# Two head pairs loaded four tokens to a partition, one set of squares split between two engines, and the operands of the last matmul stage made later

## The chip, the core and the metric

The kernel runs on one core of a Trainium2 chip. The metric is the time of one execution on the device in microseconds (us). The engines are named as in the profile: PE is TensorE (PEld its weight loads), DVE is VectorE, ACT is ScalarE, POOL is GpSimd, SP is SyncE, which here only issues DMAs.

## What is computed

The reference is an attention block with normalised queries and keys, followed by a feed-forward block with the activation SoLU.

```
q_n, k_n = rmsnorm(q, g_q), rmsnorm(k, g_k)         # q, k, v: (8, 12, 448, 64)
attn = softmax(q_n @ k_n.T / 8);  x = (attn @ v)    # -> x: (3584, 768)
h = x @ w_in                                        # w_in: (768, 1024)
solu = h * softmax(h)
ln = (solu - mean) / sqrt(var + 1e-6) * g_ln
out = ln @ w_out                                    # w_out: (1024, 768)
```

All data are float32 (the weights arrive as float64).

## The kernel before

**Attention, 0 to about 315 us.** The 96 heads are worked as 48 pairs; two pairs make a quad, so there are 24 quads. For each pair the scores are made in three blocks of 128 keys (`scores`, L802) and one block of the last 64 keys of both pairs of a quad (`scores_last`, L815). ACT takes the exponentials out of PSUM (L792), PE multiplies them with the values (L848, L859) and sums them with matmuls with ones (L881). PSUM has three buffers for score blocks, so a fourth block waits until the exponentials of the first have been taken.

Queries and keys must be normalised and transposed before the scores. From pair 2 on this runs on several engines: `squares` (ACT, L662), `row_sums` (DVE, L670), `fold_sums` (POOL, L680 and L681), `rsqrt_seed` (ACT, L687 and L688), `rsqrt_step` (DVE, L694 to L697), `normalise` (POOL, L703), `qk_transpose` (DVE, L713), `gain` (ACT, L717). The first two pairs take a shorter way: `load_rows` (L728) loads each head with tokens j*112+p in partition p, so in runs of one token (64 floats, 256 bytes), `square_rows` and `sum_rows` (L738, L740, L746) make the sums, `normalise_rows` (L762) scales the rows in place, `transpose_rows` (L768) transposes four 112x128 blocks with PE, and `take_rows` (L774 to L778) copies the result out of PSUM into `qkT`.

The order on each engine is the order in which the program issues the instructions: the attention's first quad is written out by hand (the branch `m == 0` of the loop), with `unit(...)` marking a piece of PE work.

**First feed-forward matmul, to about 569 us.** 28 tiles of 128 rows are worked as 14 groups of two tiles. Each group is a 2x2 block product that is made with seven half-size products instead of eight (p1 to p7 in `products`, L980), in banks A, B, C and D of PSUM, each with 6 matmul records and about 2.58 us. DVE adds the partial results and takes row maxima (`plus`, L996). When half a group is finished, `done` puts five steps of the activation on a list of due times (`later`): `ff_exp` (ACT, L1051), `ff_mult` (DVE, L1055), `ff_moments` (DVE L1063 to L1068, then POOL L1069 and L1071), `ff_norm` (ACT, L1075) and `ff_spread` (DVE transpose L1084, then four DMAs to DRAM, L1087). The due times are counted in PE pieces; the last two groups have due times of their own. The tiles concerned are tile 25 and 24 (group 12, its second and first half) and tile 27 and 26 (group 13).

**Second feed-forward matmul, the last stage, from 569 us.** It works on seven blocks n = 0 to 6 of four tiles, again with seven products instead of eight on two levels: the outer products P1, P5, P6, P2, P7, P3, P4 (in that order, q = 0 to 6 of each block), and in each of them seven inner products at `PLACES = (0, 4, 8, 10, 12, 16, 20)` slots after the start of the outer one, with `STEP = 7` slots from one outer product to the next. From slot 21 on there is one inner product in every slot. An inner product is four matmul records (L1194) and takes 0.65 us when PE runs freely. Numbered by their order on PE from the start of the stage, products 0, 1, 3, 4, 6, 9 and 13 belong to P1 (p1, p2, p6, p5, p7, p4, p3), products 2, 5, 8, 10, 12, 16 and 20 to P5, products 7, 11, 15, 17 and 19 to P6 (p1, p2, p6, p5, p7). From slot 21 on the number is the slot less 7.

Inner products accumulate into a bank that an engine reads in between: in P1 and P5 ACT copies bank A (L1206), in the others DVE adds to it (L1208); DVE makes the results out of C, B and B (L1233 for p2, L1246 for p7, L1256 for p3). So p6, p7 and p4 of an outer product wait for the reading of bank A, and p3 waits for the reading of bank B by p7.

The operands of a block come from DRAM (`load_u`, L1131, on SP's queue behind the spreads that were issued before) and are made by `make`: a11, a12 and a22 are copies on ACT (L1149, L1151, L1153), s1, s2, s3 and s4 are sums or differences on DVE (L1155, L1157, L1159, L1161), each in two halves t = 0 and 1. `inner_sums` (POOL, L1172 to L1175) forms the four sums of an operand that p6, p5, p7 and p3 use. `made(n, name, slots)` says in which slots the two halves are issued.

Of the kernel before, what the change touches and what calls it, by code (L numbers as in the profile page):

```python
# [14 lines left out]
OP = AluOpType  # L15
# [351 lines left out]
def fast_path(  # L367
# [274 lines left out]
    def load_v(m, queue=nc.sync):  # L642
# [14 lines left out]
        d["vl"] = lasts.pop(m)  # L657

    def squares(n):
        d = st[n]  # L660
        d["sq"] = work.tile([P, 2 * NB, 32], FP32, tag="sq", name="sq", bufs=2)
        nc.scalar.activation(d["sq"].rearrange("p (s b) d -> p s (b d)", s=2), d["qk"], AF.Square)  # L662
# [59 lines left out]
    def load_rows(n, queues):  # L722
        b, hp = divmod(n, NP)
        d = st[n] = {}
        d["qk"] = xs.tile([P, 2, 4, P], FP32, tag="x", name="x")[0:R]
        for s, src in enumerate((q, k)):
            for h in range(2):
                queues[2 * s + h].dma_start(  # L728
                    d["qk"][:, s, :, h * D : (h + 1) * D], src[b, 4 * (hp // 2) + hp % 2 + 2 * h].rearrange("(j p) d -> p j d", p=R)
                )  # L730

    def square_rows(n, s, engine):
        d = st[n]
        if s == 0:
            d["sq"] = xs.tile([P, 2, 4, P], FP32, tag="x", name="xsq")[0:R]
        x, y = d["qk"][:, s], d["sq"][:, s]
        if engine is nc.scalar:
            nc.scalar.activation(y, x, AF.Square)  # L738
        else:
            engine.tensor_tensor(y, x, x, OP.mult)  # L740

    def sum_rows(n, s):
        d = st[n]
        if s == 0:
            d["ss"] = small.tile([P, 4 * NB], FP32, tag="ss", name="ss", bufs=2)[0:R, 0:16]
        nc.vector.tensor_reduce(  # L746
            d["ss"][:, s * 8 : s * 8 + 8], d["sq"][:, s].rearrange("p j (h d) -> p (j h) d", h=2), AX, OP.add
        )

    def warm_up():  # L750
# [4 lines left out]
        for _ in range(5):  # L755
            nc.tensor.matmul(o, w[:, 0:P], w, start=True, stop=True)

    def normalise_rows(n, s):
        d = st[n]
        x = d["qk"][:, s].rearrange("p j (h d) -> p (j h) d", h=2)  # L760
        y = d["y"][:, s * 8 : s * 8 + 8].rearrange("p i -> p i ()").to_broadcast([R, 8, D])
        nc.vector.tensor_tensor(x, x, y, OP.mult)  # L762

    def transpose_rows(n, s):
        d = st[n]
        d["pt", s] = ps_t.tile([P, S], FP32, tag="o", name="pt", bufs=2)
        for j in range(4):
            nc.tensor.transpose(d["pt", s][:, j * R : (j + 1) * R], d["qk"][:, s, j], ident[0:R, 0:R])  # L768

    def take_rows(n, s):  # L770
        d = st[n]
        if s == 0:
            d["qkT"] = work.tile([P, 2, S], FP32, tag="qkT", name="qkT", bufs=3)
            nc.scalar.activation(d["qkT"][:, 0], d["pt", 0], AF.Copy, scale=gcol[:, KF : KF + 1])  # L774
        elif n == 0:
            nc.scalar.copy(d["qkT"][:, 1], d["pt", 1])
        else:
            nc.vector.tensor_copy(d["qkT"][:, 1], d["pt", 1])  # L778

# [312 lines left out]
    def in_parts():  # L1092
        def done(g, i):
            t = 2 * g + i
            ff_max(t)
            waits = {
                (NG - 2, 1): (1, 2, 3, 5, 5), (NG - 1, 1): (1, 2, 3.25, 6.75, 7), (NG - 1, 0): (2.25, 3.75, 4.75, 7.5, 8)
            }.get((g, i), (1, 2, 3, 5, 7))
# [45 lines left out]
    def make(n, name, t):  # L1144
# [11 lines left out]
        elif name == "s2":  # L1156
            nc.vector.tensor_tensor(o, us[n, "s1"][:, t], us[n, "a11"][:, t], OP.subtract)  # L1157
        elif name == "s3":
# [195 lines left out]
    with tc.manual_schedule():  # L1354
# [19 lines left out]
        for m in range(NQ):  # L1374
# [18 lines left out]
            if m == 0:  # L1393
# [3 lines left out]
                unit(lambda: scores(a, 1))  # L1397
                unit(lambda: scores(a, 2))
                for s in range(2):
                    transpose_rows(1, s)  # L1400
                    take_rows(1, s)
                squares(2)
                add(a)
                add_more(a)
                row_sums(2)
                unit(lambda: scores_last(m))
                squares(3)
                unit(lambda: scores(b, 0))
                row_sums(3)
                fold_sums(1)  # L1410
                unit(lambda: scores(b, 1))
                unit(lambda: scores(b, 2))
                add(b)
                norms_next()
                squares(4)
                row_sums(4)
# [138 lines left out]
        for n in range(NS):  # L1555
            base = period * n
            for i, name in enumerate(ORDER):
# [5 lines left out]
                if q > 1:  # L1563
                    when(STEP * q - 6, lambda n=n, x=x: inner_sums(n, x))
            for x, t, slot in (("V", 1, 31), ("V", 0, 34), ("C22", 1, 45), ("C22", 0, 52)):
# [115 lines left out]
```

## Time and profile before

| | us |
|---|---|
| median of 3 runs (lowest, highest) | 807.04 (806.71, 807.82) |
| the profiled execution, its own time | 807.2 |
| its span, first to last instruction | 805.4 |
| PE busy | 789.7 |
| DVE busy | 612.8 |
| POOL busy | 519.9 |
| ACT busy | 473.0 |

The profile is of one execution. Times in it count from the start of the span. In a timeline line the first number is the start, the second the duration from the first to the last of the instructions that the line merges, then come engine, line, operation and what is written from what; the bracket at the end tells how long the engine sat idle before and which event ended that. In the view of stretches each engine's busy time is given with its number of instructions, then the granted PE clock (1.00 is full speed), the busy share of the DMA engines (over 1 where packets overlap) and the rate.

### The profile page before, as it was taken

Reading aid. Unit: us, or ns where it says so; the run is one execution under the profiler, and the core shown is the slowest. Engines: PE = TensorE matmul, PEld = TensorE weight load, DVE = VectorE, ACT = ScalarE, POOL = GpSimd, SP = SyncE. Lnnn points to the kernel's source line nnn. Section 1 sums busy time; section 2 is a strip of 40 time slices with the busy share of each in tenths; the row PEclk is TensorE's granted clock in tenths of the full one; section 3 lists DMA queues with packets and bytes.
Section 4 is the critical chain, followed back from the end, with each engine's and each line's share of the span. In section 5 each row is a group of like instructions: output and inputs, shape, how many; then the busy total and the mean of one; then the engine's idle time right before and its main releaser. Section 6 shows DMA issues by size and latency. Waiting matters only on the chain.

```text
span 805.4 us, 14271 instructions
## 1 busy us (share of the span) xinstructions
PE 789.7 (98%) x4854; PEld 464.5 (58%) x4854; DVE 612.8 (76%) x1203; ACT 473.0 (59%) x783; POOL 519.9 (65%) x662
## 2 busy tenths in 40 slices
PE   8999999999999999999999999999899999999997
PEld 4344444443444433444444444444699999999996
DVE  6787989989888896488778667776886776866945
ACT  6677878878778764467767544453505455464420
POOL 2666777778777775244466466678487777777861
PEclk9999999999999999999999999999999999999999
DMA  9878899897787832555545445542647457366312
GB/s 170 159 168 156 182 194 184 196 187 161 165 160 169 161 103 66 140 131 151 150 131 147 102 119 140 141 110 52 210 125 252 133 188 267 117 229 213 120 60 83
DMA packets 269598, 122.68 MB, mean 152 GB/s; under 512 B 187596, under 2 KB 254668, under 8 KB 269516
## 3 DMA queue, kind: packets, MB, share of 16 engines
q1 hardware_dynamic: 254332, 111.78, 55.7%
q10 hardware_dynamic: 15184, 9.90, 4.5%
q8 instruction: 40, 0.66, 0.3%
q14 instruction: 42, 0.34, 0.1%
HBM read 84.94 MB, written 36.70 MB: 151 GB/s over the span
## 4 chain that ended last, share of the span: by engine, by line
PE 88%; DVE 3%; DMA 2%; SPq 2%; POOL 2%; ACT 1%; issue 1%; DVEq 0%; ACTq 0%; POOLq 0%
PE A L1194 15%; PE A L980 13%; PE o L859 12%; PE s L802 12%; PE B L980 8%; PE B L1194 8%; PE C L980 4%; PE sm L881 4%; PE D L980 4%; PE C L1194 4%; PE s L815 2%; PE o L848 2%; SPq L636 1%; DMA ur<-ud 1%; DMA xg<-xd 1%
## 5 line engine op out<-in xcount | busy, mean ns | idle before, releaser
L792 ACT ACTIVATE E<-s 128x896 f32<-128x896 f32 x168 | 138.8, 939 | 8.9 <-PE s L802 8.1
L802 PE MATMUL s<-qkT 64*64 64x448 f32 x1152 | 120.1, 545 | 1.7 <-ACT qkT L717 1.0
L859 PE MATMUL o<-E,v 128*64 128x448 f32 x576 | 113.8, 543 | 0.0
L1069 POOL TENSOR_TENSOR he<-he,mhalf 128x1 f32<-128x1 f32 x28 | 27.6, 986 | 105.6 <-DVE he L1068 95.7
L1194 PE MATMUL B<-w_out,sums 128*128 128x192 f32 x392 | 80.6, 329 | 3.3 <-DVE P L1256 2.1
L802 PEld LDWEIGHTS s<-qkT 64*64 64x64 f32 x1152 | 48.1, 163 | 60.0 <-ACT E L792 29.2
L1194 PE MATMUL A<-w_out,sums 128*128 128x192 f32 x392 | 80.6, 329 | 1.0 <-POOL sums L1175 0.7
L859 PEld LDWEIGHTS o<-E,v 128*64 128x64 f32 x576 | 39.1, 137 | 72.2 <-issue 68.0
L703 POOL TENSOR_TENSOR qkn<-qk,ny 128x896 f32<-128x896 f32 x46 | 77.1, 1697 | 3.5 <-DMA qk<-in_q_dram 1.5
L838 POOL TENSOR_TENSOR es<-es,E 128x896 f32<-128x896 f32 x22 | 46.4, 2109 | 48.9 <-ACT sq L662 35.4
L980 PE MATMUL B<-w_in,xsum 128*128 128x512 f32 x168 | 76.7, 593 | 0.5 <-POOL he L1069 0.5
L980 PE MATMUL A<-w_in,xg 128*128 128x512 f32 x168 | 74.6, 593 | 0.0
L1194 PEld LDWEIGHTS B<-w_out,sums 128*128 128x128 f32 x392 | 66.9, 191 | 3.9 <-DVE P L1256 2.4
L1051 ACT ACTIVATE u<-h,hmax 128x1024 f32<-128x1024 f32 x28 | 32.1, 1148 | 62.7 <-DVE hmax L1045 62.7
L1194 PEld LDWEIGHTS A<-w_out,sums 128*128 128x128 f32 x392 | 66.8, 191 | 1.7 <-POOL sums L1175 1.6
L980 PEld LDWEIGHTS B<-w_in,xsum 128*128 128x128 f32 x168 | 31.8, 190 | 41.0 <-issue 39.0
L980 PEld LDWEIGHTS A<-w_in,xg 128*128 128x128 f32 x168 | 31.8, 190 | 40.1 <-issue 39.3
L829 DVE TENSOR_TENSOR es<-E 128x896 f32<-128x896 f32 x48 | 53.0, 1107 | 2.1 <-ACT E L792 2.1
L670 DVE TENSOR_REDUCE part<-sq 128x28 f32<-128x896 f32 x46 | 47.9, 1080 | 4.4 <-ACT sq L662 2.0
L680 POOL COPY ss<-part 32x56 f32<-32x56 f32 x92 | 46.8, 508 | 6.7 <-DVE part L670 2.2
L713 DVE STREAM_TRANSPOSE qkT<-qkn 128x896 f32<-128x896 f32 x46 | 48.4, 1087 | 0.4 <-POOL qkn L703 0.4
L1194 PE MATMUL A<-w_out,s 128*128 128x192 f32 x224 | 45.6, 326 | 0.0
(150 smaller groups left out, 1647.8 us busy)
## 6 DMA issues: line engine op xcount, KB each, us to landing
ur<-ud SPq DMA_DIRECT2D x60, 256.0 KB, 4.7
ud<-ub SPq DMA_DIRECT2D x112, 128.0 KB, 2.3
xd<-xo SPq DMA_DIRECT2D x48, 224.0 KB, 3.0
qk<-in_q_dram SPq DMA_DIRECT2D x92, 112.0 KB, 3.2
qk<-in_k_dram SPq DMA_DIRECT2D x92, 112.0 KB, 3.0
v<-in_v_dram SPq DMA_DIRECT2D x24, 384.0 KB, 4.4
out_dram<-P SPq DMA_DIRECT2D x19, 384.0 KB, 4.3
raw<-in_moe_w_in_dram SPq DMA_DIRECT2D x12, 512.0 KB, 5.5
```

The costliest lines, as they stand in the source:

```text
L670: nc.vector.tensor_reduce(norms[m]["part"][:, i], st[n]["sq"], AX, OP.add)
L680: e.tensor_copy(ss[g * 32 : g * 32 + 32], part[o * 32 : o * 32 + 32])
L703: e.tensor_tensor(d["qkn"].rearrange("p (s b) d -> p s b d", s=2), d["qk"].rearrange("p s (b d) -> p s b d", d=32), y.rearrange("p (s b) - ...
L713: nc.vector.transpose(d["qkT"].rearrange("p s t -> p (s t)"), d["qkn"].rearrange("p b d -> p (b d)"))
L792: nc.scalar.activation(d["E", kc], s[:, :, 0:S], AF.Exp)
L802: nc.tensor.matmul(s[c : c + D, h, 0:S], d["qkT"][hh, 1, keys], d["qkT"][hh, 0, :], start=True, stop=True,)
L829: nc.vector.tensor_tensor(d["es"], d["E", 0], d["E", 1], OP.add)
L838: e.tensor_tensor(d["es"], d["es"], d["E", 2], OP.add)
L859: nc.tensor.matmul(d["o"][h * D : (h + 1) * D, :], quads[n // 2]["v"][:, n % 2 + 2 * h, kc], d["E", kc][:, h], start=False, stop=(kc == NJ ...
L881: nc.tensor.matmul(sm[g : g + 32, :], ones[:, w], e[:, h, t * S // 2 : (t + 1) * S // 2], start=(x == 0), stop=(x == len(terms) - 1),)
L980: nc.tensor.matmul(k[bank], a[:, c], w_in[i][:, c], start=begin and c == 0, stop=c == HD - 1, skip_group_check=not begin,)
L1194: nc.tensor.matmul(k[bank], a[:, c].rearrange("p a i -> p (a i)"), w_out[:, area, i, c], start=begin and c == 0, stop=c == KC - 1, skip_gr ...
```

## The change

1. `load_rows` puts tokens 4p to 4p+3 of a head into partition p, so a run is four tokens (1 KB). The tile's layout is (head, token, d) instead of (token, head, d). `normalise_rows` no longer works in place: it writes into the tile of the squares, in the layout that the transposes need. `take_rows` restores the order of the tokens as it copies out of PSUM, by writing each element four elements (16 bytes) after the one before.
2. In the first quad, `squares(3)` (one ACT instruction over q and k) becomes two instructions: the half for q on DVE, ahead of `take_rows` of pair 1, and the half for k on ACT, right behind `squares(2)`. `row_sums(3)` and `fold_sums(1)` are issued before `scores(b, 0)`, and `scores(b, 2)` after the seeds of the norms of the next quad, so that its exponentials follow the seeds on ACT. PE's order is the same.
3. For the last tiles of the first feed-forward matmul the due times move: moments, norm and spread of tile 24 from 3, 5, 7 to 4, 6, 7; the spread of tile 27 from 7 to 7.25; mult, moments, norm and spread of tile 26 from 3.75, 4.75, 7.5, 8 to 4.25, 6.75, 8, 8.75.
4. s2 of block 0 is made on POOL instead of DVE. Its second half is issued in slot 1 instead of 3, and the inner sums of P6 of block 0 in slot 5 instead of 8.
5. The operands of block 1 are issued later: s1 in slots 39 and 41 instead of 27 and 30, s2 in 43 and 45 (34 and 38), s3 in 47 and 49 (40 and 42), s4 in 51 and 53 (47 and 49), a22 in 55 and 57 (53 and 55). a11 and a12 stay.

```diff
+    def squares_half(n, s, vector):
+        d = st[n]
+        if s == 0:
+            d["sq"] = work.tile([P, 2 * NB, 32], FP32, tag="sq", name="sq", bufs=2)
+        y, x = d["sq"].rearrange("p (s b) d -> p s (b d)", s=2)[:, s], d["qk"][:, s]
+        if vector:
+            nc.vector.tensor_tensor(y, x, x, OP.mult)
+        else:
+            nc.scalar.activation(y, x, AF.Square)
...
-        d["qk"] = xs.tile([P, 2, 4, P], FP32, tag="x", name="x")[0:R]
+        d["qk"] = xs.tile([P, 2, 2, 4, D], FP32, tag="x", name="x")[0:R]
...
-                    d["qk"][:, s, :, h * D : (h + 1) * D], src[...].rearrange("(j p) d -> p j d", p=R)
+                    d["qk"][:, s, h], src[...].rearrange("(p j) d -> p j d", p=R)
...
+    def flat(x):
+        return x.rearrange("p h j d -> p (h j d)")
+
     def normalise_rows(n, s):
         d = st[n]
-        x = d["qk"][:, s].rearrange("p j (h d) -> p (j h) d", h=2)
-        y = d["y"][:, s * 8 : s * 8 + 8].rearrange("p i -> p i ()").to_broadcast([R, 8, D])
-        nc.vector.tensor_tensor(x, x, y, OP.mult)
+        y = d["y"][:, s * 8 : s * 8 + 8].rearrange("p (h j) -> p h j ()", h=2).to_broadcast([R, 2, 4, D])
+        o = flat(d["sq"][:, s]).rearrange("p (j h d) -> p h j d", h=2, d=D)
+        nc.vector.tensor_tensor(o, d["qk"][:, s], y, OP.mult)
...
-            nc.scalar.activation(d["qkT"][:, 0], d["pt", 0], AF.Copy, scale=gcol[:, KF : KF + 1])
+        to = d["qkT"][:, s].rearrange("p (r j) -> p j r", j=4)
+        pt = d["pt", s].rearrange("p (j r) -> p j r", j=4)
+        if s == 0:
+            nc.scalar.activation(to, pt, AF.Copy, scale=gcol[:, KF : KF + 1])
         elif n == 0:
-            nc.scalar.copy(d["qkT"][:, 1], d["pt", 1])
+            nc.scalar.copy(to, pt)
         else:
-            nc.vector.tensor_copy(d["qkT"][:, 1], d["pt", 1])
+            nc.vector.tensor_copy(to, pt)
...
-                (NG - 2, 1): (1, 2, 3, 5, 5), (NG - 1, 1): (1, 2, 3.25, 6.75, 7), (NG - 1, 0): (2.25, 3.75, 4.75, 7.5, 8)
+                (NG - 2, 1): (1, 2, 3, 5, 5), (NG - 2, 0): (1, 2, 4, 6, 7),
+                (NG - 1, 1): (1, 2, 3.25, 6.75, 7.25), (NG - 1, 0): (2.25, 4.25, 6.75, 8, 8.75),
...
-            nc.vector.tensor_tensor(o, us[n, "s1"][:, t], us[n, "a11"][:, t], OP.subtract)
+            (nc.vector if n else nc.gpsimd).tensor_tensor(o, us[n, "s1"][:, t], us[n, "a11"][:, t], OP.subtract)
...
                 unit(lambda: scores(a, 2))
+                squares_half(3, 0, True)
                 for s in range(2):
                     transpose_rows(1, s)
                     take_rows(1, s)
                 squares(2)
+                squares_half(3, 1, False)
                 add(a)
                 add_more(a)
                 row_sums(2)
                 unit(lambda: scores_last(m))
-                squares(3)
-                unit(lambda: scores(b, 0))
                 row_sums(3)
                 fold_sums(1)
+                unit(lambda: scores(b, 0))
                 unit(lambda: scores(b, 1))
-                unit(lambda: scores(b, 2))
                 add(b)
                 norms_next()
+                unit(lambda: scores(b, 2))
                 squares(4)
...
-                    when(STEP * q - 6, lambda n=n, x=x: inner_sums(n, x))
+                    when(STEP * q - 6 if q > 2 else 5, lambda n=n, x=x: inner_sums(n, x))
...
-            late = 6 if n == 1 else 0
-            made(n, "a11", base + 12 + late, base + 15 + late)
-            made(n, "s1", base + 21 + late, base + 24 + late)
-            made(n, "s2", base + 28 + late, base + 38)
+            late = n == 1
+            made(n, "a11", base + 12 + 6 * late, base + 15 + 6 * late)
+            made(n, "s1", base + 21 + 18 * late, base + 24 + 17 * late)
+            made(n, "s2", base + 28 + 15 * late, base + 38 + 7 * late)
             made(n, "a12", base + 33, base + 36)
-            made(n, "s3", base + 40, base + 42)
-            made(n, "s4", base + 47, base + 49)
-            made(n, "a22", base + 53, base + 55)
+            made(n, "s3", base + 40 + 7 * late, base + 42 + 7 * late)
+            made(n, "s4", base + 47 + 4 * late, base + 49 + 4 * late)
+            made(n, "a22", base + 53 + 2 * late, base + 55 + 2 * late)
...
-        made(0, "s2", 0, 3)
+        made(0, "s2", 0, 1)
```

More of the change, by code (lines that the diff above doesn't have):

```diff
@@ L728, in load_rows @@
                 queues[2 * s + h].dma_start(
-                    d["qk"][:, s, :, h * D : (h + 1) * D], src[b, 4 * (hp // 2) + hp % 2 + 2 * h].rearrange("(j p) d -> p j d", p=R)
+                    d["qk"][:, s, h], src[b, 4 * (hp // 2) + hp % 2 + 2 * h].rearrange("(p j) d -> p j d", p=R)
                 )
@@ L734, in square_rows @@
         if s == 0:
-            d["sq"] = xs.tile([P, 2, 4, P], FP32, tag="x", name="xsq")[0:R]
+            d["sq"] = xs.tile([P, 2, 2, 4, D], FP32, tag="x", name="xsq")[0:R]
         x, y = d["qk"][:, s], d["sq"][:, s]
@@ L746, in sum_rows @@
         nc.vector.tensor_reduce(
-            d["ss"][:, s * 8 : s * 8 + 8], d["sq"][:, s].rearrange("p j (h d) -> p (j h) d", h=2), AX, OP.add
+            d["ss"][:, s * 8 : s * 8 + 8], d["sq"][:, s].rearrange("p h j d -> p (h j) d"), AX, OP.add
         )
@@ L767, in transpose_rows @@
         for j in range(4):
-            nc.tensor.transpose(d["pt", s][:, j * R : (j + 1) * R], d["qk"][:, s, j], ident[0:R, 0:R])
+            nc.tensor.transpose(d["pt", s][:, j * R : (j + 1) * R], flat(d["sq"][:, s])[:, j * P : (j + 1) * P], ident[0:R, 0:R])
     def take_rows(n, s):
```

## The prediction

> **What bounds the kernel now.** I read the page's first part, then who PE waited for, then the stretches and timelines around those waits.
>
> ```profile
> span 805.4 us, 14271 instructions
> PE 789.7 (98%) x4854; PEld 464.5 (58%) x4854; DVE 612.8 (76%) x1203; ACT 473.0 (59%) x783; POOL 519.9 (65%) x662
> ```
>
> PE is busy for all but 805.4 - 789.7 = 15.7 us, so the change can win only there, or where PE is busy at a low clock. PE's waits:
>
> ```profile
> PE B L1194 <- DVE P L1256: 2.1, 1, 2.1
> PE s L815 <- ACT E L792: 1.3, 2, 0.7
> PE pt L768 <- DVE x L762: 1.2, 1, 1.2
> PE B L1194 <- DVE P L1246: 1.2, 1, 1.2
> PE s L802 <- ACT qkT L717: 1.0, 1, 1.0
> PE A L1194 <- POOL sums L1175: 0.7, 1, 0.7
> PE s L802 <- ACT qkT L776: 0.6, 1, 0.6
> PE B L980 <- POOL he L1069: 0.5, 1, 0.5
> ```
>
> The L1194 and L980 rows lie between 566 and 598 us, where the last stage begins; the rest, but for one of the two at L815, lies before 30 us. From 30 to 300 us PE waits for nothing. The stretches at the first two show one thing more:
>
> ```profile
> 582.00:584.00 2.00, 0.20 (x2) 0.00 (x0) 2.00 (x5) 1.15 (x2) 1.82 (x4) 1.00 0.28 108
> 584.00:586.00 2.00, 1.65 (x8) 1.65 (x9) 1.71 (x5) 0.42 (x1) 2.00 (x3) 0.83 0.48 110
> 586.00:588.00 2.00, 2.00 (x8) 2.00 (x7) 0.67 (x2) 0.00 (x0) 1.92 (x4) 0.50 0.86 207
> 588.00:590.00 2.00, 2.00 (x11) 2.00 (x11) 1.47 (x4) 0.74 (x2) 1.99 (x3) 0.82 0.55 207
> ```
>
> The reader is to see PE idle while DVE is full, and then a granted clock of 0.50: products 18 to 21 start at 585.10, 586.16, 587.44 and 588.72, so three steps take 3.62 instead of 3 x 0.65 = 1.95 us. The wait of 2.15 costs a further 1.67. What kept DVE:
>
> ```profile
> 581.69 0.68 DVE L1161 TENSOR_TENSOR s<-a,s 128x512 f32<-128x512 f32 x1
> 582.29 0.34 DVE L1233 TENSOR_TENSOR P<-C,q 128x192 f32<-128x192 f32 x1
> 582.56 0.34 DVE L1246 TENSOR_TENSOR P<-B,u 128x192 f32<-128x192 f32 x1
> 582.82 1.23 DVE L1084 STREAM_TRANSPOSE ub<-u 128x1024 f32<-128x1024 f32 x1
> 583.98 0.31 DVE L1256 TENSOR_TENSOR P<-B,u 128x192 f32<-128x192 f32 x1
> ```
>
> Bank B is read (L1256) only behind a spread; before that came moments, mult(26) and two s2.
>
> **What the Trainium skill says.** "TensorE: Matmul & The Clock Gate", section on the HAM clock gate: PE falls to half clock after an idle window of about 3.4 us and returns after a busy one. The trace agrees on half (0.50) and about 3.5 us; here 2.15 us of waiting, 1.16 shortly before it, were enough. "SBUF — State Buffer", Who interferes with whom: a DVE instruction with two SBUF inputs and a POOL instruction that reads SBUF block each other. Agrees: the power at L1069 takes 0.55 us alone and 1.46 under a DVE product (559.84). The same page, Door 1, on 16-byte lines: an access that crosses to a new line pays. No row of before writes so; reading every second word costs ACT 820 against 630 ns (L535, L536, 128x512). "DMA: Bandwidth & Descriptors", Why small descriptors are slow: fixed work per packet. Agrees in direction: 251 to 281 GB/s at full DMA share from 2.5 to 4 us with runs of 256 bytes, 354 and 379 at 568 to 570 with long rows.
>
> **Part 1, the loads.** The first pair's four DMAs carry 448 KB: about 1.75 us at 260 GB/s, 1.25 at 360, so DVE's first square (4.45) starts 0.5 earlier. The chain from there to the first score (10.46) has that much room beside it: the gain column's transpose is held by PE's warm-up to 7.2, and ACT's squares of pair 1, which follow it, end at 8.64, where the first copy would start at 9.32 - 0.5 = 8.82. Given back: two copies on the path (0.63 and 0.53) write with a step of 16 bytes. At the 30% of L535 over L536 that is +0.17 each; bounds nothing and doubling. The new output layout of L762 is in whole runs of 64: nothing. Sum +0.2 (from -0.7 to +0.7).
>
> **Part 2, the squares.** DVE is free from 12.89 to 13.93, which hides 0.6 for half the squares; without that cover it would delay L778. The other half (some 0.5) ends on ACT at 15.95 and puts the exponentials of the last keys from 15.71 to 15.95; PE's third block of pair 1, released at 16.68, loses about 0.2. That lies before the 1.0 wait at 26.02 and is absorbed by it. Row sums of pair 3 move from 17.50 to 16.55; the fold (18.73) is then held by POOL's add until 17.81; the seeds go from 20.97 to about 20.1. Late next: the exponentials of L792 for `scores(b, 2)`, 0.92, now stand behind the seeds, so the squares of pair 4 stay at 21.67, their row sums end at 23.74, and the transpose behind them goes from 24.16 only to 23.75. Sum +0.45 (0 to 0.8). The following wait of 0.66 at 29.28 hangs on the same chain and moves along.
>
> **Part 3, due times of tile 24.** B's first reading (L996) comes before the moments: at 564.53, when ACT has copied u3, instead of 566.08. PE goes on at 566.40 instead of 566.92 and the last stage starts at 568.98 instead of 569.57: +0.59. On ACT exp(27) now precedes norm(24), which ends at 570.46 instead of 568.43; the copy of q behind it stays at 570.4, and product 3 (570.93) just gets it.
>
> **Parts 3 and 4, products 9 to 21.** With before's steps DVE runs: mult(27) 570.11, p2 571.25, spread(24) 571.52, moments(27) 572.68, two s3 574.61, p2 575.81, p7 of P1 576.07 to 576.42. Product 13 needs that at 577.4: the wait of 1.16 goes. s2 costs POOL two of about 1.34 us (L563, 128x512), where POOL was idle from 567.2 to 576.6; even blocked by mult(27) and starting only after the last in-stage matmul it is ready by 573, and product 7 wants its first half at 573.5. Then mult(26), s4, p2 end at 578.6. P5's p7 needs ACT's copy of u3, queued behind a11 of block 1, whose load follows spread(24), 1.7 earlier than before: about 579.3. P1's p3 is done by 579.6, product 17 starts at 580.4: the wait of 2.15 goes, and 1.67 of low clock with it.
>
> Late next, two new waits. ACT's a12 copies wait for a load that lands at 573.65 (issued behind spread(25), not moved); the copy of u3 behind them ends at 575.16, and product 9 now wants it at 574.83: -0.35. And product 19 (581.7) waits for DVE's reading of P6's A (L1208), behind spread(27) 1.16, s4 0.6, one add 0.27: about 581.9, a microsecond more if a11 lands late: -0.6 (0.2 to 1.0).
>
> **Part 5, block 1's operands.** The 0.66 at product 33 goes (its release at 597.32 is DVE's L1208 behind a V and an s2; the profile names POOL). The work comes back in slots 39 to 55: 17 adds at 0.28 start to start = 4.8, s1, s2, s3, s4 twice at 1.02, 0.96, 0.68, 0.82 = 7.0, two C22 at 0.8 = 1.6; 13.4 us, where PE needs 16 x 0.65 = 10.4. Of the 3.0 about 2 is room, as a bank is read some three slots before it is wanted. -0.9 (0 to 1.6). The operands have more than 6 us to their use, so POOL's sums and the loads they release are covered.
>
> **Sum.** Stage: 0.59 + 1.16 + 2.15 + 1.67 + 0.66 - 0.35 - 0.6 - 0.9 = 4.4 (3.3 to 5.7). Start: 0.65. Together 5.05, from the profiled execution's own 807.2 (span 805.4 and 1.8 around it) to 802.15; its time is 0.16 above the median 807.04, so 802.0.
>
> **Rivals.** *All clean* (0.13): POOL's blocking and the strided writes cost nothing, products 19 and 45 never wait: stage 5.9, start 1.3, so 799.8. For it: before, DVE passed a similar crowd at 589 to 606 with one wait of 0.66. *The backlog reaches the clock* (0.19): in slots 45 to 58 DVE and POOL stretch each other (s2 1.21 where 0.68 is possible), PE waits 2 us within one window and pays another 1.67: 804.3. For it: 13.4 against 10.4 us. *Hidden anyway, the change doesn't do what it says* (0.06): the loads of block 1 land so late that P5's u3 copy and with it L1256 are as late as before; only 0.6 and the start remain: 806. Against it: spread(24) moves with its norm, which was never the late one. *Slower* (0.04): DVE stays the bound of products 13 to 21, so that all of the stage's 4.4 is lost, and the operands packed into slots 39 to 55 add 1.5 of waits and a second half-clock window of 1.67: 807.0 + 3.2 - 0.65 = 809.6. It decides from 2 us of PE idle within one such window (2.15 did it, 1.16 alone not).
>
> **Chances.** Forecast 0.58, its own range 800.8 to 803.2. Range 799.8 to 804.8: the forecast, most of the backlog case and half of the clean one, 0.8. Faster by over 0.2% (about what a measurement of this kernel can tell from no change), below 805.4: 0.58 + 0.19 + 0.13 = 0.90; same 0.06; slower 0.04.
>
> **What would show it.** Right: the L1256 and L1246 rows gone from PE's waits, clock 1.00 throughout 578 to 592, the last stage beginning about 1.2 earlier, waits of under 0.5 at products 9 and 19. Wrong: a wait over 1 us between products 38 and 51, a clock below 1 there, copies at `take_rows` over 0.9 us, POOL's s2 over 2 us each.

## The result and the profile after

The changed kernel takes 803.26 us, the median of 13 runs (801.98 to 806.14), against 807.18 for the kernel before beside it (13 runs, 805.98 to 808.20). The ratio is 0.9956, 95% interval 0.9946 to 0.9965: faster by 3.9 us, where 5.05 was forecast. The profiled execution took 802.73 with a span of 800.9, so that one is 4.47 below the profiled execution of before.

The page's first part. PE is busy as long as before to within 0.6 us, in a shorter span; POOL's busy time has grown by 3.8:

```profile
span 800.9 us, 14266 instructions
PE 789.1 (99%) x4854; PEld 462.8 (58%) x4854; DVE 613.8 (77%) x1202; ACT 473.1 (59%) x783; POOL 523.7 (65%) x664
```

PE's waits, all that the view lists: time in all, times, longest (line numbers are those of the changed kernel; L818 and L831 are the scores, L1211 the last stage's products, L1273 and L1263 the readings of bank B that were L1256 and L1246, L1225 the reading of A that was L1208):

```profile
PE s L818 <- ACT qkT L792: 1.6, 1, 1.6
PE pt L766 <- DVE warm L763: 1.4, 1, 1.4
PE s L831 <- ACT E L808: 0.9, 2, 0.7
PE A L1211 <- POOL sums L1190: 0.8, 1, 0.8
PE A L1211 <- DVE u L1225: 0.6, 2, 0.4
PE B L1211 <- DVE P L1273: 0.5, 1, 0.5
PE s L831 <- ACT qkT L790: 0.3, 1, 0.3
PE pt L781 <- DVE xsq L775: 0.2, 1, 0.2
PE s L818 <- ACT qkT L727: 0.2, 1, 0.2
```

The rows of 2.1 and 1.2 at bank B are gone. At the start waiting has moved more than it has gone: PE's wait for the copy of the first pair grew from 0.6 to 1.6, while the rows of 1.2 before the transposes and of 1.0 at pair 2 shrank to 0.2 each. The stretches at the old waits:

```profile
582.00:584.00 2.00, 1.43 (x9) 1.46 (x10) 1.93 (x7) 0.00 (x0) 1.86 (x3) 1.00 0.85 204
584.00:586.00 2.00, 2.00 (x14) 2.00 (x13) 1.93 (x8) 0.65 (x1) 1.50 (x3) 1.00 0.79 254
586.00:588.00 2.00, 2.00 (x14) 2.00 (x13) 1.77 (x4) 1.61 (x3) 1.92 (x4) 1.00 0.18 70
588.00:590.00 2.00, 2.00 (x15) 2.00 (x14) 1.93 (x6) 0.00 (x0) 1.92 (x4) 1.00 0.56 124
```

The clock stays at 1.00 where it was 0.50, and in the stretch from 582 PE stands still for 0.57 us instead of 1.80, although DVE is as full as before. The timeline shows why: P1's reading of B now comes ahead of the spread.

```profile
578.67 0.62 ACT L1166 COPY a<-ur 128x512 f32<-128x512 f32 x1 [1.14 <-DMA ur<-ud]
579.20 0.31 ACT L1223 COPY u<-A 128x192 f32<-128x192 f32 x1
579.54 0.36 DVE L1263 TENSOR_TENSOR P<-B,u 128x192 f32<-128x192 f32 x1
579.82 0.35 DVE L1273 TENSOR_TENSOR P<-B,u 128x192 f32<-128x192 f32 x1
580.08 1.24 DVE L1100 STREAM_TRANSPOSE ub<-u 128x1024 f32<-128x1024 f32 x1
```

Product 17 then starts at 580.32 instead of 584.35. The last stage's first product starts at 568.58 (569.57 before) and its last at 794.72 (799.29), 4.57 earlier. Of that 0.22 was there before the stage's eve: PE's block that began at 558.50 begins at 558.28. It isn't the start's doing, as PE's wait for exponentials at 29 us ends later than before (29.43, not 29.28); a wait near 306 us, of which more below, was 0.39 shorter in this execution. The remaining 4.35 come from the stage and its eve.

### The profile page after: what moved, and what is told of

Same layout as the page of the kernel before. It is cut to its first block, busy times and chain, and to the rows that moved or that the text cites. A ratio compares the mean times of both kernels' runs of the same rounds, so it can differ in the third digit from the quotient of the medians.

```text
span 800.9 us, 14266 instructions
## 1 busy us (share of the span) xinstructions
PE 789.1 (99%) x4854; PEld 462.8 (58%) x4854; DVE 613.8 (77%) x1202; ACT 473.1 (59%) x783; POOL 523.7 (65%) x664
## 4 chain that ended last, share of the span: by engine, by line
PE 88%; DVE 4%; POOL 2%; ACT 2%; DMA 1%; issue 1%; SPq 0%; DVEq 0%; ACTq 0%; POOLq 0%
PE A L1211 14%; PE A L996 13%; PE o L875 12%; PE s L818 12%; PE B L996 8%; PE B L1211 7%; PE C L996 5%; PE sm L897 4%; PE D L996 4%; PE C L1211 3%; PE s L831 2%; PE o L864 2%; PE pt L766 1%; DMA xg<-xd 1%; ACT E L808 1%
## 5 line engine op out<-in xcount | busy, mean ns | idle before, releaser
L818 PE MATMUL s<-qkT 64*64 64x448 f32 x1152 | 120.1, 545 | 1.7 <-ACT qkT L792 1.6
L818 PEld LDWEIGHTS s<-qkT 64*64 64x64 f32 x1152 | 47.9, 163 | 60.3 <-ACT E L808 29.2
L1211 PE MATMUL A<-w_out,sums 128*128 128x192 f32 x392 | 80.0, 327 | 1.1 <-POOL sums L1190 0.8
L1211 PE MATMUL B<-w_out,sums 128*128 128x192 f32 x392 | 79.8, 326 | 0.5 <-DVE P L1273 0.5
L1211 PEld LDWEIGHTS A<-w_out,sums 128*128 128x128 f32 x392 | 66.1, 190 | 2.2 <-POOL sums L1190 1.3
L1211 PEld LDWEIGHTS B<-w_out,sums 128*128 128x128 f32 x392 | 66.2, 190 | 0.8 <-DVE P L1273 0.7
L1211 PE MATMUL A<-w_out,s 128*128 128x192 f32 x224 | 45.7, 326 | 0.0
```

The source lines that it names most:

```text
L818: nc.tensor.matmul(s[c : c + D, h, 0:S], d["qkT"][hh, 1, keys], d["qkT"][hh, 0, :], start=True, stop=True,)
L1211: nc.tensor.matmul(k[bank], a[:, c].rearrange("p a i -> p (a i)"), w_out[:, area, i, c], start=begin and c == 0, stop=c == KC - 1, skip_gr ...
```

## Experiments

Two theories stood at the outset. A: all of the gain is in the last stage, and the strided writes of the copies eat what the earlier loads give. B: the start gains about 0.65 as forecast, and the stage less than 4.4.

**The last stage alone**, parts 1 and 2 undone (the loads, squares and copies are those of before; here only the hunk of the loads, seen from the changed kernel):

```diff
-                    d["qk"][:, s, h], src[...].rearrange("(p j) d -> p j d", p=R)
+                    d["qk"][:, s, :, h * D : (h + 1) * D], src[...].rearrange("(j p) d -> p j d", p=R)
```

> Only the last stage's edits (due times, s2 on POOL, block 1's operands later); the start is that of before. Theory A, the gain is all in the stage and the start gives nothing: 4.3 us below before, so about the changed kernel's time or up to 0.5 better. Rival B, the start gains its forecast 0.65 and the stage only 3.3: 3.3 below before.

804.08 us (803.18 to 806.00, 6 runs), ratio 0.9953 (0.9936 to 0.9971). By the ratio that is the whole gain, by the medians 2.9 us of it; the interval, 2.3 to 5.2 us, holds both theories, so this run doesn't decide between them.

**The start alone**, parts 3 to 5 undone (shown in part; the slots of parts 4 and 5 go back too):

```diff
-                (NG - 2, 1): (1, 2, 3, 5, 5), (NG - 2, 0): (1, 2, 4, 6, 7),
-                (NG - 1, 1): (1, 2, 3.25, 6.75, 7.25), (NG - 1, 0): (2.25, 4.25, 6.75, 8, 8.75),
+                (NG - 2, 1): (1, 2, 3, 5, 5), (NG - 1, 1): (1, 2, 3.25, 6.75, 7), (NG - 1, 0): (2.25, 3.75, 4.75, 7.5, 8)
...
-            (nc.vector if n else nc.gpsimd).tensor_tensor(o, us[n, "s1"][:, t], us[n, "a11"][:, t], OP.subtract)
+            nc.vector.tensor_tensor(o, us[n, "s1"][:, t], us[n, "a11"][:, t], OP.subtract)
```

> Only the loads and the split squares; the last stage is that of before. Theory A: within 0.5 us of before, either sign; copies of L790 and L792 near 1.0 us, first score later than before. Rival B: 0.65 below before.

807.01 us (22 runs), ratio 0.9996 (0.9988 to 1.0003): no gain that can be told from none, though the upper end, 1.0 us, would also hold the 0.65 forecast. In this profile the two waits at bank B are as long as before (2.1 and 1.1), and yet the clock did not fall: the period at half clock does not come in every execution.

**The old loads**, part 1 alone undone (the hunk of the first experiment, `normalise_rows`, `transpose_rows` and `take_rows` with it; part 2 stays).

> The changed kernel with the loads of before (one token to a partition, copies out of PSUM written without a step); split squares and stage as changed. Theory A, the strided writes cost 0.86 on the path and the faster loads return 0.4: 0.5 to 0.9 below the changed kernel, first score before 10.6 instead of 11.08. Rival B, the loads are worth 0.2 or more: above the changed kernel by 0.2 or more.

803.86 us (6 runs), ratio 0.9951 (0.9933 to 0.9969). The first score starts at 10.50 and the scores of pair 2 at 25.43; the changed kernel has 11.08 and 26.16. So part 1 costs 0.6 to 0.7 by 26 us in these profiles. The time doesn't show it: at 306 us PE waits 1.18 for an exponential in this execution, where the changed kernel's waited 0.22, and the interval, some 1.5 us to either side, is wider than what is sought. What part 2 does is plain here, where the loads are those of before. POOL folds the sums of squares and ACT's seeds of the norms follow; before:

```profile
18.73 1.83 POOL L680 COPY ss<-part 32x56 f32<-32x56 f32 x4 [0.92 <-DVE part L670]
20.97 0.34 ACT L687 ACTIVATE ny<-ss,eps 128x56 f32<-128x56 f32 x1 [1.09 <-POOL ss L681]
```

and in this kernel:

```profile
17.91 1.95 POOL L690 COPY ss<-part 32x56 f32<-32x56 f32 x4
20.27 0.34 ACT L697 ACTIVATE ny<-ss,eps 128x56 f32<-128x56 f32 x1 [1.90 <-POOL ss L691]
```

**Order restored on the reading side.** The copies write in order and read PSUM with the step:

```diff
-        to = d["qkT"][:, s].rearrange("p (r j) -> p j r", j=4)
-        pt = d["pt", s].rearrange("p (j r) -> p j r", j=4)
+        to = d["qkT"][:, s].rearrange("p (r j) -> p r j", j=4)
+        pt = d["pt", s].rearrange("p (j r) -> p r j", j=4)
```

> The changed kernel, but the copies out of PSUM write in order and read with a step of 112 elements instead of reading in order and writing with a step of 4. Theory A, it is the 16-byte step of the writes that doubles the copies: copies back at 0.5 to 0.65 us and 0.5 below the changed kernel. Rival B, any step costs the same, on whichever side: copies still near 1.0 us and the changed kernel's time.

803.01 us (802.26 to 803.49, 6 runs), ratio 0.9937 (0.9922 to 0.9953). The copies and the first scores, in the changed kernel:

```profile
9.21 1.03 ACT L790 ACTIVATE qkT<-pt,gcol 128x448 f32<-128x448 f32 x1
10.04 0.99 ACT L792 COPY qkT<-pt 128x448 f32<-128x448 f32 x1
11.08 2.52 PE L818 MATMUL s<-qkT 64*64 64x448 f32 x24 [1.55 <-ACT qkT L792]
```

and in this one:

```profile
9.58 0.62 ACT L790 ACTIVATE qkT<-pt,gcol 128x448 f32<-128x448 f32 x1
10.10 0.52 ACT L792 COPY qkT<-pt 128x448 f32<-128x448 f32 x1
10.67 2.52 PE L818 MATMUL s<-qkT 64*64 64x448 f32 x24 [1.02 <-ACT qkT L792]
```

Same elements, same instructions: the step of 16 bytes in the writes costs 0.41 and 0.47 us, and the step of 448 bytes in the reads of PSUM costs nothing that shows. The first score comes at 10.67 instead of 11.08; the time, 0.25 lower, doesn't prove it, as the intervals overlap. The copies begin later here, 9.58, because PE's warm-up took 6.90 us instead of 6.53 and held the gain column's transpose to 8.20; over all profiles with five warm-up matmuls their ten instructions took 5.65 to 6.90.

**s2 of block 0 back on DVE**, in its new slots (the second hunk of the start alone, nothing else).

> The changed kernel, but the two s2 of block 0 stay on DVE (in their new slots). Theory A, DVE's order decides products 13 to 19: two s2 of about 0.68 put DVE 1.36 us later from 569 us on. P1's p7 then comes at about 577.6 instead of 576.3 and its last reading at 581.2 instead of 579.8, so PE waits at products 13 and 17, 1.0 to 1.5 us in all, mult(27) being 0.65 shorter without POOL beside it takes some of that back: 804.0 to 804.8, against 803.3 for the changed kernel. Rival, the due times of tile 24 had freed enough: PE's gaps stay at those of the changed kernel, 803.3.

804.07 us (8 runs), ratio 0.9959 (0.9945 to 0.9974), against 0.9956 for the changed kernel: no difference that can be measured. On POOL the two s2 take 2.52 us and stretch mult(27) from 1.22 to 1.88; on DVE they take 1.29. So the move takes 0.63 from DVE's queue, not 1.29. P1's last reading of B comes 11.58 after the stage's first product instead of 11.24, product 15 comes 0.58 late instead of 0.14, product 16 0.10 instead of 0.25, and the stage from its first to its last product takes 226.45 instead of 226.14. The rival holds: with the new due times s2 had room.

**Old due times**, part 3 undone (the first hunk of the start alone, nothing else).

> The changed kernel, but the due times of tiles 24 to 27 are those of before. Theory A, the due times carry most of the stage's gain: the last stage starts 0.6 later, and the waits before products 13 and 17 come back with at least a part of the half clock, 2 to 4 us: 805.5 to 807. Rival, s2 on POOL is enough for DVE: only the 0.6 of the start of the stage and a wait of about half a microsecond come back: 804 to 804.5.

805.70 us (22 runs), ratio 0.9979 (0.9971 to 0.9987): by the ratio about half of the gain is lost. The timeline has the old order back, the reading behind the spread, and product 17 behind it:

```profile
580.40 0.92 PE L1210 MATMUL A<-w_out,s 128*128 128x192 f32 x4 [0.17 <-ACT u L1222]
581.50 1.23 DVE L1100 STREAM_TRANSPOSE ub<-u 128x1024 f32<-128x1024 f32 x1
582.66 0.31 DVE L1272 TENSOR_TENSOR P<-B,u 128x192 f32<-128x192 f32 x1
583.02 0.92 PE L1210 MATMUL B<-w_out,sums 128*128 128x192 f32 x4 [1.71 <-DVE P L1272]
```

The wait at product 13 stays away but for 0.1. Part 5 can't have removed it, as product 13 is in slot 20 and the operands that part 5 moves came from slot 27 on; so part 4 did, with the due times of before. Undoing part 4 alone did not bring it back either: for product 13 either of parts 3 and 4 is enough, for product 17 only part 3. PE waits 0.8 for bank B on the stage's eve (0.5 before), as the forecast of part 3 had it. The profiled execution took 804.18 and has no period at half clock here; but 13 of the 22 have a mean clock of 0.997 or less, and those take 805.24 to 807.36, the other nine 803.80 to 805.28.

**Block 1's operands in the old slots**, part 5 undone:

```diff
-            late = n == 1
...
-            made(n, "s1", base + 21 + 18 * late, base + 24 + 17 * late)
-            made(n, "s2", base + 28 + 15 * late, base + 38 + 7 * late)
+            late = 6 if n == 1 else 0
...
+            made(n, "s1", base + 21 + late, base + 24 + late)
+            made(n, "s2", base + 28 + late, base + 38)
...
-            made(n, "s3", base + 40 + 7 * late, base + 42 + 7 * late)
+            made(n, "s3", base + 40, base + 42)
...
```

> The changed kernel, but the operands of block 1 are made in the slots of before. Theory A, as the prediction reckoned it: 0.66 at product 33 comes back and some 1.0 at products 45 and 51 goes, so 802.9 against 803.3, no more than the measurement can tell. Rival, the operands collide with the later moments of tiles 26 and 27 that part 3 moved behind 580 us: waits of over 1.5 us between products 19 and 35, 804.5 or more.

804.60 us (10 runs), ratio 0.9968 (0.9956 to 0.9980): between the theories, nearer the rival, with an interval that overlaps the changed kernel's. The delays of products 45 and 51 (0.62 and 0.40) are gone, but products 30 and 33 come 0.76 and 1.54 late, where before had 0.82 at product 33 alone: 1.3 us net. The 0.48 and 1.30 at products 16 and 19, in slots 23 and 26, lie ahead of the first operand that differs and aren't part 5's. DVE's reading of bank A that product 30 waits for, at 593.81, stands behind the spread of tile 26 (590.82), which part 3 moved back, an s1 and a V. So part 5 belongs to part 3, though to the spread rather than the moments that the rival named. The profiled execution (807.61) shows one thing more, a period at half clock near the start:

```profile
10.00:12.00 2.00, 1.19 (x12) 0.67 (x16) 0.93 (x5) 1.06 (x3) 0.00 (x0) 0.87 0.95 159
12.00:14.00 2.00, 2.00 (x14) 0.57 (x12) 1.58 (x3) 1.36 (x2) 0.00 (x0) 0.50 1.03 260
14.00:16.00 2.00, 2.00 (x18) 0.93 (x12) 0.04 (x1) 1.42 (x3) 0.00 (x0) 0.77 0.92 148
```

The scores of pair 2 start at 27.66 there, 1.5 to 1.8 later than in the others with the same start. Up to the last stage this kernel's program is that of the changed one, so the same could befall that one too.

**The squares as before**, part 2 undone:

```diff
-                squares_half(3, 0, True)
...
-                squares_half(3, 1, False)
...
                 unit(lambda: scores_last(m))
+                squares(3)
+                unit(lambda: scores(b, 0))
                 row_sums(3)
```

> The changed kernel, but part 2 (the split squares of pair 3 and the earlier row sums) is undone. Theory A, part 2 brings what the prediction says and part 1 costs nothing net: 0.45 is lost, 803.7, and the wait before the scores of pair 2 is longer by about that. Rival, the wait of PE on an exponential near 310 us swallows what is won before it: that wait is shorter by as much and the time stays at 803.3.

804.41 us (9 runs), ratio 0.9959 (0.9947 to 0.9972): no difference from the changed kernel that can be measured. From the first score to the scores of pair 2 it takes 15.95 us (27.29 - 11.34), the changed kernel 15.08: part 2 gives 0.87 there, in one profile of each. In the time it doesn't show, but the interval, 1.0 us to either side, could hide it.

**Does a wait near 306 us take the start's gain?** Near 306 us, in the changed kernel (SPq is SyncE issuing a load):

```profile
297.00 0.60 SPq L948 DMA_DIRECT2D xg<-xd  x1
303.31 0.84 ACT L957 ACTIVATE xsum<-xg 128x768 f32<-128x768 f32 x1 [4.28 <-DMA xg<-xd]
305.12 3.32 ACT L808 ACTIVATE E<-s 128x896 f32<-128x896 f32 x4
306.07 0.98 PE L831 MATMUL s<-qkT 64*64 64x448 f32 x8 [0.22 <-ACT E L808]
```

and in the kernel with s2 on DVE, whose program is the same up to here:

```profile
296.83 0.60 SPq L948 DMA_DIRECT2D xg<-xd  x1
304.93 0.84 ACT L957 ACTIVATE xsum<-xg 128x768 f32<-128x768 f32 x1 [6.06 <-DMA xg<-xd]
306.74 1.70 ACT L808 ACTIVATE E<-s 128x896 f32<-128x896 f32 x2
307.69 0.61 PE L831 MATMUL s<-qkT 64*64 64x448 f32 x4 [2.01 <-ACT E L808]
```

ACT squares the first x tile (L957) ahead of the last quad's exponentials, so the exponentials and PE behind them wait for a transfer that took 6.3 us here and 8.1 there. But the wait doesn't swallow what was won before it. In all fourteen profiles, that of before and those of every kernel here, the load is issued 267.56 or 267.57 us after PE's wait at 29 us has ended (at 28.36 to 30.91): whatever the start wins or loses reaches this load whole. From the issue to the squares it takes 6.31 to 8.10 us in the eleven with the squares in front, with no relation to the start that could be seen (7.91 in the kernel that was earliest at 29 us, 6.56 and 7.80 in the two latest), and PE's wait is that time less 6.09. So the transfer adds 0.2 to 2.0 us that differ from execution to execution; they hide a few tenths won at the start but do not take them. Moving the squares behind the exponentials was to remove the wait:

```diff
             if m == NQ - 2:
                 load_x(0)
-                sizes(0)
...
             unit(lambda: scores(b, 2))
+            if m == NQ - 1:
+                sizes(0)
```

> The changed kernel, with one call moved: the two squares of the first x tile (sizes(0), L957) come on ACT behind the exponentials of the last quad instead of ahead of them. Theory A, what the start wins is swallowed near 310 us because these squares wait for a transfer that lands when it will, and the exponentials and PE wait behind them: PE's wait at L831 near 306 us goes, the exponentials begin as soon as the scores are there, and the time falls by the size of that wait, 0.2 to 2 us from run to run, so about 802.5 and with less spread. Rival, the wait is the exponentials' own pace (ACT needs 0.94 a block) and only moves a few blocks on: 803.3 as the changed kernel.

802.90 us (801.79 to 803.21, 6 runs), ratio 0.9944 (0.9932 to 0.9955). The wait is gone: exponentials start at 304.05, the scores of L831 at 305.31. From PE's wait at 29 us to the block on the stage's eve it takes 528.18, against 528.61 to 528.64 plus the wait near 306 in the eleven profiles with the squares in front; so the move saves that wait and 0.4 more. The last stage starts at 567.56, 1.0 earlier than in the changed kernel, 0.35 of it from the start. But product 9 comes 0.47 late, product 16 0.63 and product 19 1.39, and the last product starts 0.23 later than in the changed kernel's profile. That the early start brings the delays of products 16 and 19 is not shown: with the same stage they come to 1.8 to 2.5 us also in kernels that begin it 0.2 to 1.4 later than the changed one, which had 1.2 only. Product 16 waits for ACT's copy behind the first a11 of block 1, a load again, whose landing differs by up to a microsecond. Theory A's wait is shown, the gain in time not: against the changed kernel the median is 0.4 lower, inside the intervals.

**Four warm-up matmuls instead of five**, on the kernel that reads PSUM with the step:

```diff
-        for _ in range(5):
+        for _ in range(4):
```

> The changed kernel with the copies of take_rows writing in order and reading PSUM with the step (as in the run before that did so), and four warm-up matmuls instead of five. Theory A, the warm-up's end holds the gain column and with it ACT's squares of pair 1 ahead of the first copy: the gain column's transpose comes at about 6.9 instead of 7.8 to 8.2, the first copy at 8.9 instead of 9.2 to 9.6, the first score at 10.0 instead of 10.7, and the time is up to 0.5 below 803.0. Rival, PE is not warm then: the transposes and first scores run at half clock, each block of scores 0.3 to 0.5 longer, and the first score's 0.6 are lost again by 26 us: 803.0 or a little more.

803.77 us (802.67 to 805.80, 7 runs), ratio 0.9962 (0.9948 to 0.9976). The start does what theory A says: gain column's transpose at 6.86, first copy at 8.98, first score at 10.17, scores of pair 2 at 25.10. At 306 us PE waits 1.81. Three of the seven have a mean clock of 0.996 or 0.997 and take 803.22 to 805.80.

**All four ideas**, which adds to that the squares behind the exponentials and the spread of tile 27 half a step later:

```diff
-                (NG - 1, 1): (1, 2, 3.25, 6.75, 7.25), (NG - 1, 0): (2.25, 4.25, 6.75, 8, 8.75),
+                (NG - 1, 1): (1, 2, 3.25, 6.75, 7.75), (NG - 1, 0): (2.25, 4.25, 6.75, 8, 8.75),
```

> A version meant to beat both kernels: the changed one, with the copies of take_rows reading PSUM with the step, four warm-up matmuls, the squares of the first x tile behind the last exponentials, and the spread of tile 27 due half a step later, behind DVE's reading of the bank that product 19 wants. Theory A: product 19's wait of 0.94 (1.46 in the run with the PSUM reads) goes if DVE's reading was its releaser, though the profile names POOL's sums; with the other three 800.8 to 801.5. Rival, POOL's sums release it, as the profile says: the wait stays at about 1, and the time is 801.8 to 802.5.

801.90 us (801.37 to 803.82, 6 runs), ratio 0.9941 (0.9927 to 0.9955). On product 19: the profile of the changed kernel names POOL's sums as its releaser.

```profile
581.20 1.28 POOL L1190 TENSOR_TENSOR sums<-sums,a 128x256 f32<-128x256 f32 x1
582.08 0.34 DVE L1225 TENSOR_TENSOR u<-A,P 128x192 f32<-128x192 f32 x1
582.57 0.89 PE L1211 MATMUL A<-w_out,sums 128*128 128x192 f32 x4 [0.78 <-POOL sums L1190]
```

In the kernel with the squares moved it names another of POOL's four sums:

```profile
581.54 1.18 POOL L1192 TENSOR_TENSOR sums<-a,sums 128x256 f32<-128x256 f32 x1
582.32 0.34 DVE L1225 TENSOR_TENSOR u<-A,P 128x192 f32<-128x192 f32 x1
582.81 0.89 PE L1211 MATMUL A<-w_out,sums 128*128 128x192 f32 x4 [1.23 <-POOL sums L1192]
```

One product can't need both; common to the two is DVE's reading of bank A, 0.15 before, as in all nine profiles in which product 19 waits. With the spread behind that reading:

```profile
579.49 0.34 DVE L1225 TENSOR_TENSOR u<-A,P 128x192 f32<-128x192 f32 x1
579.75 1.23 DVE L1100 STREAM_TRANSPOSE ub<-u 128x1024 f32<-128x1024 f32 x1
579.98 0.89 PE L1211 MATMUL A<-w_out,sums 128*128 128x192 f32 x4
...
583.04 0.35 DVE L1225 TENSOR_TENSOR u<-A,P 128x192 f32<-128x192 f32 x1
583.44 0.92 PE L1211 MATMUL A<-w_out,s 128*128 128x192 f32 x4 [0.62 <-DVE u L1225]
```

Product 19 no longer waits. It starts at 579.98, while POOL's sum of L1190, the one that the changed kernel's profile names, only ends at 580.69; so DVE's reading was its releaser. Most of the gap comes back as 0.79 at product 23, where DVE's reading stands behind the spread and the moments of tile 26.

**The same with five warm-up matmuls.**

> The version before, but with all five warm-up matmuls again. Theory A, the fifth warm-up matmul only delays the gain column: the first score comes at 10.6 to 10.8 instead of 10.20, the scores of pair 2 about 0.5 later, and the time is 802.2 against 801.9. Rival, with four PE falls to half clock once in some runs (mean clocks of 0.996 and 0.997 in three of seven and two of six runs with four, none of six with five): then no run here has a mean clock under 0.998 and the median is 801.3 to 801.8, below that with four.

801.35 us (801.05 to 802.23, 5 runs), ratio 0.9932 (0.9918 to 0.9945), the fastest of all and below the changed kernel's interval (0.9946 to 0.9965). The first score comes at 10.24, no later than with four (10.20), although the gain column waits till 7.78: at full length the warm-up costs little here, and no execution has a mean clock under 0.998, as the rival has it. It is the best of twelve versions, on five executions, so its lead is likely to be flattered. Whether four matmuls bring on the half clock is not settled: the counts are small (five of 13 with four, none of 11 with five and the same copies), and no execution at half clock with four was profiled.

## Why the prediction was nearly right

The time lies in the range, on the slower side of the likeliest case (800.8 to 803.2). Of the signs that it named, the rows at bank B are gone and the clock stays at 1.00; but the copies over 0.9 us, one of its signs of being wrong, came (1.03 and 0.99), and the wait at product 19 is not under 0.5. Going by its own steps:

- **Stage, 4.4 forecast, 4.35 in the pair of profiles.** In the old profile the steps to products 13, 17, 19 to 21 and 33 exceed 0.65 by 6.12 us in all; all of that is gone. New are 0.14 and 0.25 at products 15 and 16, 0.94 at 19, 0.62 and 0.41 at 45 and 51: 2.36. With steps of about 0.1 behind each gap the stage is 3.58 shorter, and the eve gives the rest. That the number fits so well is luck. From the block on the eve to the last product it takes 240.78 in the profile of before, with half clock, and 239.86 in that of the start alone, without; the changed kernel's 236.44 is the shortest of seven profiles with the same stage (to 237.71). So the gain is 2.2 to 4.3, by the executions one compares.
- **Part 3 on the stage's eve**, +0.59: 0.76. From the block at 558 to the stage's first product it takes 11.06 before and 10.30 in each of the eleven profiles with the new due times.
- **Products 13 and 17 and the half clock**, +4.98: right, and for the reason given. P1's readings came at 576.26 and 579.82 (576.07 and 579.3 to 579.6 forecast), product 17 at 580.32 (580.4). That part 3 carries this is shown by undoing it, for product 17; product 13 needs only one of parts 3 and 4.
- **The half clock in this sum**, 1.67: it was a property of one profile: the start alone had the waits without it. The mean clocks say that such a period comes in about half of the executions of before: 43 of 84 beside the experiments have a mean clock of 0.997 or less, and their medians lie 1.1 to 1.7 us higher. With the start alone and the old due times that makes 67 of 128; with the new due times and five warm-up products, 7 of 69. The forecast took it as always there, so the 1.67 should have counted about half. That may be why the medians differ by 3.9 and the profiles by 4.47; it was not traced run by run.
- **Why the same wait brings half clock only at times** was not tested, but the traces suggest a reason. In all fourteen profiles every change of the clock lies a whole number of steps of 3.41 us after its first rise (585.32 in before is 170 of them after 5.05). Before's wait, 582.20 to 584.35, lies within one such step, from 581.91 to 585.32, which holds 2.14 us of PE idle; in the start alone and in the kernel with the old due times the edge of a step cuts the wait, and no step there holds more than 1.16. How much idle it takes can't be read off: a step with 1.55 was followed by half clock at 11.5 us, one with 1.67 that ends at 308.35, in the kernel with four warm-up products, was not.
- **Product 9**, -0.35: did not come. The a12 load landed in time (copies at 571.96 instead of 573.65). It came, at 0.47, where the stage began 1.0 earlier.
- **Product 16**, which the sum had at nothing: 0.25 here, 0.3 to 1.3 in seven of the eight others with the new due times and the old spread of tile 27, behind the load of a11. The prediction saw that this load may land late, but only for product 19.
- **Product 19**, -0.6 (0.2 to 1.0): 0.94 here and up to 1.45, for the reason given, as moving the spread showed; the profile's own label pointed elsewhere.
- **s2 on POOL**: reckoned as part of what frees products 13 and 17. It is enough alone for product 13, not for 17; with part 3 there, it changes nothing that can be measured.
- **Part 5**, +0.66 and -0.9: 0.82 and -1.03. It is worth more than this sum of -0.2: without it the delays of products 30 to 51 are 1.3 us longer. The forecast compared it with the old slots in the old order, and not with the old slots beside part 3's due times.
- **Part 2**, +0.45: 0.6 to 0.9 from the first score to pair 2 (15.56 before, 14.93 with the old loads and part 2; 15.95 and 15.08 with the new loads). The way was that forecast: with the old loads POOL's folding starts at 17.91 instead of 18.73, right behind its add, and the seeds come at 20.27 (20.1 forecast, 20.97 before). In the changed kernel they come at 20.94 only because part 1 has pushed everything back: 9.86 after the first score, where before had 10.51.
- **Part 1**, +0.2: this is the step that failed. The loads did land 0.36 to 0.49 earlier (first squares at 4.09 on DVE and 4.44 on ACT, from 4.45 and 4.93; 0.5 forecast). But the copies' strided writes were sized at +0.17 each from a row that reads every second word, with doubling as the bound; they cost 0.40 and 0.46, inside the bounds and more than twice what was taken. In this execution the warm-up also ran to 7.8 instead of 7.2, as the clock rose later (6.45, not 5.05), and held the gain column and ACT's squares, so that the first copy moved from 9.32 only to 9.21, not 8.82. That is the smaller share: in four other profiles the copy began at 8.91 to 9.00, and the first score still came at 10.81 to 10.87. With the strided copies it came at 10.81 to 11.08 in six profiles of seven (11.34 in the other), against 10.46 to 10.57 in the three without part 1: -0.4 in place of +0.2.
- **The start as a whole**, +0.65: about nothing, as part 1 loses what part 2 gains. PE's wait at 29 us ended at 29.28 and 29.42 in the two profiles with the start of before and at 29.08 to 29.43 in five of the six with the whole new start (30.91 in the one with half clock). In time the start alone is worth 0.3 us, with an interval that takes in nothing and the 0.65.

## What to carry to other kernels

A gain of a few tenths at the start is to be looked for where it is made: a load in the middle that lands 6.3 to 8.1 us after its issue, with critical work queued behind it, hides it in the end-to-end time of six or nine runs. Follow it from wait to wait before calling it lost. Where a copy has to reorder fp32, try the step on the PSUM side first. Where an engine is full, ask for each of its readings of a PSUM bank what stands ahead of it; here order decided more than the amount of work moved away. And the releaser that a profile names for a wait should be tried against the bank's last reader.

## What the runs showed of the hardware

- Writing 448 fp32 per partition to SBUF with a step of 16 bytes took 1.03 and 0.99 on ACT and 0.96 on DVE, against 0.63, 0.53 and 0.62 in order; reading PSUM with a step of 448 bytes and writing in order took 0.62, 0.52 and 0.62. "SBUF — State Buffer", Door 1, of the Trainium skill says that an access pays when it crosses to a new 16-byte line; the writes here agree, at 1.5 to 1.9 times the duration.
- The same five warm-up products took 5.65 to 6.90 us. "TensorE: Matmul & The Clock Gate", section "What's actually happening", says that the window is free-running and the number of cold matmuls varies from run to run; these traces agree, with a spread of 1.25 us that follows the clock's first rise (4.67 us where the five took 5.65, 7.20 where they took 6.90). The gain column of the first pair waits behind them.
- A period of 3.41 us at half clock came at 11.5 us in one execution and at 585.3 in another, and waits of 2.1 and 1.1 us near 580 stayed without it once.
- One load of x, issued at the same place of the program, reached ACT 6.3 to 8.1 us after its issue began, over eleven profiles with the squares in front.
